# A recurrent cross-attention and maxout kernel on one Trainium2 core: batch 0 loaded uncast on both hardware queues, and every order, bank and queue laid out anew

## The chip, the cores and the metric

The kernel runs on one core of one Trainium2 chip. The metric is the device time of one launch in microseconds (us), the median of several runs. A profiled execution of the same program gives a trace with the busy time of each engine: PE is TensorE (matmuls), PEld its weight loads, DVE is VectorE, ACT is ScalarE, POOL is GpSimd, SP is SyncE (which here only issues DMAs). An engine runs its instructions in the order of the program and waits on semaphores for the others.

## The reference

`x` is 8 x 8 x 512 x 64 (batch, head, position, depth), `state` is 8 x 8 x 32 x 64, both float32. Per batch and head the positions read the states and the states read the positions; then a maxout layer with three weight matrices and an output matrix runs over all 4352 rows.

```python
scores = scale * x @ state.T          # softmax over the 32 states
xread  = softmax(scores) @ state
scores2 = scale * state @ x.T         # softmax over the 512 positions
sread  = softmax(scores2) @ x
rows = concat([xread, sread], axis=2) -> (4352, 512)
h    = maximum(maximum(rows @ w1, rows @ w2), rows @ w3)   # 512 -> 768
out  = h @ w_out                                           # 768 -> 512
```

## The kernel before, in words

Compute is in bfloat16, sums in PSUM are float32. For each batch b the x tile (128 partitions x 2048) is turned so that depth lies on partitions (`xT`), scores of all heads come from matmuls against block diagonals of the states (`bd`), ScalarE takes the exponentials (`e`), VectorE sums and inverts them, and a product gives the weights `a`, which are turned (`aT`). Instead of computing xread and multiplying it with W, the kernel multiplies the states of the batch with W first (`G`, in slices of columns), so that a layer1 product is `aT` times `G`, with 2 contracted blocks. sread is a matmul of `e` with x, is scaled, turned and gathered in `atp`; its rows run through layer 1 at the end for all batches at once ("s").

The whole program is written out by hand as strings of short steps, and each step issues its instructions on a fixed engine in the order of the string. Nothing is rescheduled. FIRST covers batches 0 and 1 and the head of batch 2; EACH is performed for b = 2 to 6, with batch numbers counted from b (`gr 1` is batch b+1, `l2 -1` is batch b-1); LAST ends batches 6, 7 and the states. The letter at the end of a step names the engine that does it or the queue that a DMA goes to (D VectorE, A ScalarE, P GpSimd, S SyncE; two letters: one half each). The steps that matter here:

- loads: `lst k` two batches of states; `lxu b g` one half of the heads of x as float32, uncast, which `cxu` casts afterwards; `lxg b g` the same half cast to bfloat16 by a GpSimd DMA; `lx b` all of x; `lw m0 m1 i` columns 128*m0 to 128*m1 of W number i, cast, GpSimd; `lwo` the output matrix
- `busy n`: n matmuls on zeros; `stc`, `stt`, `stp`: states cast, turned, placed in `bd`, which `clr` clears; `xt`, `xtc`: x turned on TensorE and copied out; `xtd`, `atd`, `srt`: turned by a DMA on SP
- `sc`, `ex`, `sum`, `wt`: scores, exponentials, sums with reciprocal, weights; `at`, `atc`: weights turned and copied; `sr`, `srs`: sread and its scaling (line 323; lines 333 and 339); `pad` a copy of x that sread uses (lines 304 and 307); `ap` places the turned sread in `atp` (`sread_place`, line 347)
- `g`, `gr` with `gc`, `grc`: a slice or run of G columns (line 359) and its copy out (lines 377, 399, 402)
- `l1`: three products of one slice of 128 columns (line 412), into three PSUM banks; `m0` copies the first out on ScalarE (427), `ma` and `mb` take the maxima with the second and third on VectorE (432, 436)
- `l2` with `l2c`: an output block (443, 450); `l2p`, `l2pc`: parts of one (458, 462); `so`, `sop`, `sos`: stores (473, 468 and 466, 481); `look`, `flag`: one flag that says whether all sums lie in a safe range

PSUM has eight banks. Four are handed out singly by the digits of BANKS, in the order of the program, the other four as two pairs by PAIRS; a step that gets a bank waits until the one before it in that bank has been read. At the end the flag is read into a register of every engine, and only if it says that a sum was out of range a second, slower form of the whole computation runs; with these inputs it is skipped.

Of the kernel before, what the change touches and what calls it, by code (L numbers as in the profile page):

```python
# [15 lines left out]


FIRST = """
    zero; busy 10; clr 3; lxu 0 0 S; lxg 1 0; lst 0 A; lxg 0 1; clr 1; busy 1; stc 0 D; clr 0; ident;
    lxg 1 1; busy 2; lw 0 2 1; stt 0; lst 1 S; cxu 0 0 D; xones 0; xt 0 0; stp 0 A; busy 2; xt 1 0;  # L20
    xtc 0 0 D; sc 0 0; busy 4; warm; xtc 1 0 D; lw 0 1 2; xt 0 1; sc 1 0; lw 0 4 0; xt 1 1; ex 0 0;
    xtc 0 1 A; sc 0 1; xones 1; sum 0 0; stc 1 P; ex 1 0; lw 1 3 2; xtc 1 1 D; lw 3 5 2; ex 0 1; lw 2 3 1;
    sum 1 0; sc 1 1; stt 1; busy 6; lw 3 6 1; lxg 2 1; wt 0 0 P; ex 1 1; at 0 0; sum 0 1; sr 0; atc 0 0 A;
    clr 2; busy 1; wt 1 0 P; stp 1 A; wt 0 1 P; at 1 0; sum 1 1; at 0 1; wt 1 1 D; g 0 0; lxg 2 0; sr 1;
    atc 0 1 A; srs 1; at 1 1; g 1 0; g 1 1; gc 0 0 A; atc 1 0 D; l1 0 0; atc 1 1 A; ones; g 0 1; gc 1 0 A;
    gc 1 1 D; m0 0 0; gc 0 1 A; xtd 2; l1 1 0; g 0 2; srs 0; m0 1 0; lw 5 6 0; g 1 2; l1 1 1; ma 0 0;
    lw 5 6 2; lw 4 5 0; l1 0 1; pad 2; mb 0 0; g 1 3; gc 0 2 A; m0 1 1; gc 1 2 A; ma 1 0; lxg 3 1; g 0 3;
    l1 0 2; m0 0 1; gc 0 3 A; m0 0 2; l1 1 2; g 0 4; mb 1 0; g 0 5; ma 1 1; l1 0 3; gc 1 3 A; lst 2 A; lwo;
    mb 1 1; l1 1 3; m0 1 2; ma 0 1; g 1 4; gc 0 4 A; g 1 5; m0 0 3; gc 0 5 A; l1 0 5; mb 0 1; ma 0 2;
    m0 1 3; mb 0 2; gc 1 4 A; m0 0 5; l1 1 4; ma 1 2; mb 1 2; ma 0 3; ma 1 3; l1 0 4; mb 0 3; mb 1 3;  # L30
    ma 0 5; mb 0 5; m0 1 4; m0 0 4; gc 1 5 A; sc 2 -; lxg 3 0; ma 1 4; mb 1 4; gr 2 1024 1280; lst 3 S;
    gr 2 0 512; ex 2 -; xtd 3; l1 1 5; ma 0 4; gr 2 512 1024; grc 2 1024 1280 D; lx 4; gr 2 1792 2304;
    mb 0 4; stc 3 P; sum 2 -; grc 2 0 512 A; grc 2 1792 2304 D; stc 2 P; l2 0 2; m0 1 5; l2 0 3;
    gr 2 1280 1792; l2c 0 2 D; wt 2 - P; stt 2; grc 2 1280 1792 A; l2 0 1; grc 2 512 1024 A; ma 1 5; mb 1 5;
    l2 0 0; stp 2 D; stt 3; sr 2; stp 3 A; l2c 0 3 D; so 0 2 4 A; l2c 0 1 D; l2c 0 0 A; srs 2; so 0 0 2 P;
    atd 2;
"""
EACH = """
    gr 1 1792 2304; lx 3; gr 1 0 512; l2 -1 3; sc 1 -; grc 1 0 512 A; pad 1; l2 -1 0; ex 1 -; l1 0 0;
    l2 -1 1; grc 1 1792 2304 D; gr 1 1280 1792; gr 1 1024 1280; srt -2; xtd 2; sum 1 -; l2c -1 3 A;  # L40
    gr 1 512 1024; sr 1; l2c -1 0 A; m0 0 0; l1 0 1; ma 0 0; l1 0 2; l2c -1 1 A; so -1 0 2 A; mb 0 0;
    grc 1 1024 1280 DA; l1 0 3; srs 1; m0 0 1; m0 0 2; ma 0 1; m0 0 3; mb 0 1; wt 1 - P; l1 0 5; m0 0 5;
    l2 -1 2; grc 1 1280 1792 A; grc 1 512 1024 A; ma 0 2; l1 0 4; mb 0 2; ma 0 3; mb 0 3; ma 0 5; m0 0 4;
    mb 0 5; ma 0 4; mb 0 4; l2c -1 2 A; atd 1; ap -2 D; so -1 2 4 P;
"""
LAST = """
    srt 7; srt 5; l1 7 0; l2 6 3; l1 7 2; ap 5 A; l2 6 1; srt 6; l1 7 3; m0 7 0; ma 7 0; mb 7 0; ap 6 A;
    ap 7 D; m0 7 2; l2c 6 3 D; l2c 6 1 A; l1 7 4; m0 7 3; l1s 0; m0 7 4; ma 7 2; mb 7 2; ma 7 3; mb 7 3;
    l1 7 1; l2 6 0; m0 s 0; ma 7 4; m0 7 1; l2c 6 0 A; ma s 0; mb 7 4; ma 7 1; mb s 0; mb 7 1; l1 7 5;
    m0 7 5; l1s 2; ma 7 5; mb 7 5; m0 s 2; l2p 7 1 384 512; l1s 1; ma s 2; l2p 7 0 384 512; l2p 7 3 256 512;  # L50
    l2pc 7 1 384 512 A; l2 6 2; m0 s 1; sop 7 1 384 512 S; l2p 7 3 0 256; ma s 1; l2p 7 2 128 384;
    l2pc 7 0 384 512 D; l1s 5; l2pc 7 3 256 512 A; l2c 6 2 A; l2p 7 0 0 128; mb s 2; l1s 3; l1s 4; mb s 1;
    l2pc 7 2 128 384 D; m0 s 5; l2p 7 2 0 128; l2p 7 2 384 512; l2p 7 0 128 256; l2pc 7 3 0 256 A;
    l2p 7 1 0 128; m0 s 3; look; ma s 5; sop 7 3 256 512 S; l2pc 7 0 0 128 D; sop 7 2 128 384 S; m0 s 4;
    sop 7 0 384 512 S; mb s 5; sop 7 0 0 128 A; ma s 3; so 6 2 3 P; so 6 1 2 S; so 6 3 4 S; so 6 0 1 P;
    l2pc 7 2 0 128 A; ma s 4; mb s 3; l2p 7 0 256 384; mb s 4; l2pc 7 0 128 256 D; flag; l2p s 0 0 256;
    l2pc 7 2 384 512 A; sop 7 0 128 256 S; sop 7 2 384 512 S; l2pc 7 1 0 128 A; l2pc 7 0 256 384 D;
    l2pc s 0 0 256 D; sop 7 2 0 128 S; l2p 7 1 128 384; l2 s 1; sop 7 1 0 128 A; l2c s 1 D;
    l2pc 7 1 128 384 A; sop 7 3 0 256 S; sop 7 0 256 384 S; sop s 0 0 256 S; sop 7 1 128 384 S;
    l2p s 0 256 512; l2pc s 0 256 512 D; sos 1 A; sop s 0 256 512 S;  # L60
"""

BANKS = """
    0123012130 2310231031 3232132013 2013210321 0321302301 3203123013 0212302131 2031203120 3123013203
    1201320132 0132013210 3120132031 2031203120 3123013203 1201320132 0132013210 3120132031 2031203120
    3123013203 1201321032 0132013021 0230213021 0320323102 3021320130 120312013
"""
PAIRS = """
    0101010110 1010100010 1010010100 1010010100 10
"""  # L70


# [1 line left out]
def kernel(  # L74
# [10 lines left out]
    nc = tc.nc  # L85

    B, H, S, D = x.shape
# [35 lines left out]
    zero = const.tile([128, 512], BF16, name="zero")  # L123
    ident = const.tile([128, 128], BF16, name="ident")
    ones = const.tile([128, 128], BF16, name="ones")
    warm = const.tile([128, 1], F32, name="warm")
# [3 lines left out]
    flag = data.tile([128, 1], I32, name="flag")  # L130

    xT, e, a, aT, G, ht, osb, xp = {}, {}, {}, {}, {}, {}, {}, {}
# [176 lines left out]
    srs = {}  # L309
# [188 lines left out]
    def set_flag():  # L498
# [3 lines left out]
        nc.vector.reduce_sum(out=n, in_=p, axis=AX.X)  # L502
        nc.vector.tensor_scalar(out=flag, in0=n, scalar1=255.5, scalar2=None, op0=ALU.is_le)

# [9 lines left out]
        "gr": (g_run, 1), "grc": (g_ran, 1), "l1": (layer1, 1), "l1s": (layer1_states, 0),  # L517
        "m0": (max_first, 1), "ma": (max_second, 1), "mb": (max_third, 1), "l2": (layer2, 1), "l2c": (layer2_out, 1),
        "l2p": (layer2_part, 1), "l2pc": (layer2_part_out, 1), "sop": (store_part, 1), "so": (store, 1), "sos": (store_states, 0), "look": (look_at_sums, 0), "flag": (set_flag, 0),
    }  # L520

    def value(t):
# [38 lines left out]
    def sread_below_max(b):  # L561
# [18 lines left out]
        for g in range(2):  # L580
            p = bank([128, 2, 2, 128], BF16, "pat")
            for c in range(2):
                for i in range(2):
# [2 lines left out]
                           in_=p.rearrange("p i c k -> p (i c) k"))  # L586
        sread(b)

    bad = nc.values_load(flag[0:1, 0:1], min_val=0, max_val=1,
                         skip_runtime_bounds_check_because="flag is the result of a comparison")  # L590
    homes["b"], homes["w"] = cycle("0123"), cycle("01")
    with tc.If(bad != 0, label="again"):
        for b in range(B):
# [68 lines left out]
```

## Time and profile before

| what | us |
|---|---|
| median of 3 runs (157.18 to 157.36) | 157.34 |
| span of the profiled execution | 155.3 |
| median less span (what lies around it) | 2.04 |
| PE busy / PEld / DVE / ACT / POOL | 147.1 / 73.6 / 113.6 / 87.1 / 52.1 |
| first layer1 matmul, start | 17.02 |
| last matmul, end | about 150.1 |
| landing of the last store | about 154.4 |

The span runs from the first instruction to the last. [...] A window row gives start and end, its length, then busy time and number of instructions of PE, PEld, DVE, ACT and POOL, the granted TensorE clock, the DMA share and the rate in GB/s. A chain row gives the start, the length and what it was. A timeline row gives start, length, engine, line, operation and operands. For a casting load the trace counts the bytes written.

### The profile page before, as it was taken

To read this page: it belongs to the slowest core of one execution; us is meant where nothing else is said; L and a number is where in the kernel's file an instruction comes from. 1 tells how busy PE (TensorE), PEld (TensorE's weight loads), DVE (VectorE), ACT (ScalarE), POOL (GpSimd) and SP (SyncE) were. 2 spreads that over 40 slices of the span, in tenths; PEclk is the share of its full clock that TensorE was granted. 3 is DMA by queue.
4 is the path that set the end of the run, shared out by engine and by line. 5 is a ranking of instruction groups with operands and counts; after the bars stand their busy time and mean duration, and the time that the engine had idled before them with its cause. 6 is when DMAs were issued, how large, how long until landed. Compare 5 with 4: busy or idle time off the path is not lost.

```text
span 155.3 us, 3610 instructions
## 1 busy us (share of the span) xinstructions
PE 147.1 (95%) x1429; PEld 73.6 (47%) x1429; DVE 113.6 (73%) x196; ACT 87.1 (56%) x143; POOL 52.1 (34%) x69
## 2 busy tenths in 40 slices
PE   6989899999999999999999999999999999999960
PEld 2565333354453444444444443444344445679930
DVE  3577788799957788877687799688978767636530
ACT  0677787865486476557655865466637543333300
POOL 6999509502239007700770073106220100002000
PEclk9999999999999999999999999999999999999995
DMA  4999999999979996998499930923060300015444
GB/s 123 231 196 201 196 189 171 159 189 196 194 194 224 268 151 200 130 178 163 153 128 179 177 135 0 174 44 135 4 211 17 135 2 4 0 37 202 167 145 142
DMA packets 39477, 22.30 MB, mean 144 GB/s; under 512 B 23584, under 2 KB 37408, under 8 KB 39456
## 3 DMA queue, kind: packets, MB, share of 16 engines
q0 software_dynamic: 14944, 10.75, 40.5%
q1 hardware_dynamic: 22928, 7.47, 28.2%
q10 hardware_dynamic: 1584, 3.80, 6.8%
q8 instruction: 12, 0.20, 0.5%
q14 instruction: 9, 0.07, 0.2%
HBM read 15.20 MB, written 8.91 MB: 155 GB/s over the span
## 4 chain that ended last, share of the span: by engine, by line
PE 77%; DVE 9%; DMA 6%; POOL 4%; issue 1%; DVEq 0%; POOLq 0%
PE pw L412 45%; PE po L443 19%; DMA w<-in_moe_w_dram 6%; PE pg L359 5%; PE po L458 4%; DVE atp L347 3%; DVE ht L436 2%; PE psr L323 2%; DVE seen L272 1%; DVE G L399 1%; POOL x L166 1%; PE ps L258 1%; POOL w L177 1%; DVE t L432 1%; POOL x L194 1%
## 5 line engine op out<-in xcount | busy, mean ns | idle before, releaser
L412 PE MATMUL pw<-aT,G 128*128 128x512 bf16 x288 | 67.1, 379 | 0.0
L432 DVE TENSOR_TENSOR t<-t,pw 128x512 bf16<-128x512 bf16 (+1 forms) x54 | 35.0, 649 | 14.4 <-ACT t L427 11.8
L427 ACT CAST t<-pw 128x512 bf16<-128x512 f32 (+1 forms) x54 | 30.6, 567 | 23.8 <-PE pw L412 19.9
L412 PEld LDWEIGHTS <-G 128*128 128x128 bf16 x288 | 27.2, 98 | 33.6 <-issue 2.7
L443 PE MATMUL po<-wout,ht 128*128 128x512 bf16 x168 | 40.6, 379 | 0.0
L436 DVE TENSOR_TENSOR ht<-t,pw 128x512 bf16<-128x512 bf16 x48 | 32.9, 686 | 4.8 <-PE pw L412 0.5
L473 POOL DMA_DIRECT2D out_dram<-osb x8 | 4.8, 601 | 66.1 <-ACT osb L450 43.4
L443 PEld LDWEIGHTS <-ht 128*128 128x128 bf16 x168 | 15.3, 98 | 19.3 <-issue 2.3
L399 ACT CAST G<-pg 128x1024 bf16<-128x1024 f32 x18 | 17.7, 1019 | 4.6 <-PE pg L359 4.6
L450 ACT COPY osb<-po 128x512 f32<-128x512 f32 x24 | 13.6, 589 | 10.9 <-PE po L443 10.9
L280 POOL TENSOR_TENSOR a<-e,rden 128x1024 bf16<-128x1024 bf16 (+1 forms) x9 | 14.6, 1636 | 14.4 <-DVE rden L274 6.5
L307 POOL COPY xp<-x 128x1024 bf16<-128x1024 bf16 x12 | 12.4, 1071 | 5.3 <-DMA x<-in_x_dram 5.3
L359 PE MATMUL pg<-w,bd 64*32 64x512 bf16 (+1 forms) x288 | 12.2, 364 | 0.6 <-DMA w<-in_moe_w_dram 0.6
L272 DVE TENSOR_REDUCE seen<-e 128x32 f32<-128x1024 bf16 (+1 forms) x10 | 9.9, 990 | 3.5 <-ACT e L265 3.5
L265 ACT ACTIVATE e<-ps 128x1024 bf16<-128x1024 f32 (+1 forms) x10 | 8.4, 853 | 4.0 <-PE ps L258 2.9
L377 ACT CAST G<-pg 128x768 bf16<-128x768 f32 x11 | 8.9, 808 | 2.9 <-PE pg L359 2.9
L207 PE MATMUL idle<-zero 128*128 128x512 bf16 x26 | 8.5, 472 | 1.3 <-DVE zero L185 1.3
L412 PE MATMUL pw<-atp,w 128*128 128x256 bf16 x72 | 8.7, 273 | 0.0
L359 PEld LDWEIGHTS <-bd 64*32 64x32 bf16 x336 | 3.5, 89 | 9.0 <-issue 7.6
L177 POOL DMA_DIRECT2D w<-in_moe_w_dram x10 | 7.6, 773 | 0.4 <-DMA w<-in_moe_w_dram 0.4
L412 PEld LDWEIGHTS <-w 128*128 128x128 bf16 x72 | 7.0, 98 | 1.2
L347 DVE COPY atp<-ats 128x128 bf16<-128x128 bf16 x6 | 7.5, 1254 | 0.0
(66 smaller groups left out, 111.2 us busy)
## 6 DMA issues: line engine op xcount, KB each, us to landing
out_dram<-osb ACTq DMA_DIRECT2D x6, 512.0 KB, 5.0
out_dram<-osb POOLq DMA_DIRECT2D x6, 512.0 KB, 3.0
x<-in_x_dram POOLq DMA_DIRECT2D x4, 512.0 KB, 8.1
x<-in_x_dram POOLq DMA_DIRECT2D x7, 256.0 KB, 5.9
w<-in_moe_w_dram POOLq DMA_DIRECT2D x3, 256.0 KB, 9.2
wout<-in_moe_w_out_dram POOLq DMA_DIRECT2D x1, 768.0 KB, 9.4
out_dram<-osb SPq DMA_DIRECT2D x6, 128.0 KB, 3.0
w<-in_moe_w_dram POOLq DMA_DIRECT2D x5, 128.0 KB, 8.4
```

The lines of the kernel that those rows point to most:

```text
L272: nc.vector.reduce_sum(out=den, in_=parity(e[b], g), axis=AX.X)
L280: times[c](out=parity(a[b], g).rearrange("p j g s n -> p j (g s) n"), in0=parity(e[b], g).rearrange("p j g s n -> p j (g s) n"), in1=rdens ...
L307: nc.gpsimd.tensor_copy(out=xp[b][:, :, :, g * (D + 1):g * (D + 1) + D], in_=v[:, g])
L347: copier[c](out=atp[:, :, b // 4, :, b % 4], in_=ats[:, b])
L359: nc.tensor.matmul(p(s, g), bd(b, 2 * s + g)[64 * g:64 * g + 64, g, :], f(w_sb[64 * g:64 * g + 64, s]), start=True, stop=True, tile_positi ...
L399: copier[c[g]](out=v[:, g:h], in_=p[:, g:h, 0:c1 - c0])
L412: nc.tensor.matmul(pw[i][:, 0:n], lhs(i, k), rhs(k), start=(k == 0), stop=(k == nk - 1))
L427: nc.scalar.copy(out=t0s[b, m][:, 0:n], in_=open_ps["l", b, m][0][:, 0:n])
L432: nc.vector.tensor_max(t1s[b, m][:, 0:n], t0s.pop((b, m))[:, 0:n], open_ps["l", b, m][1][:, 0:n])
L436: nc.vector.tensor_max(ht[b][:, m, :], t1s.pop((b, m))[:, 0:n], open_ps.pop(("l", b, m))[2][:, 0:n])
L443: nc.tensor.matmul(p, ht[b][:, m, j * 128:(j + 1) * 128], wout_sb[:, m, :], start=(m == 0), stop=(m == NM - 1))
L450: copier[c[i]](out=o[:, j, i * w:i * w + w], in_=p[:, i * w:i * w + w])
```

## The change

Batch 0's x is no longer loaded half uncast by SP and half cast by GpSimd: both halves come uncast, one on SP's queue and one on ACT's, and GpSimd casts the second. W is loaded in column slices 0 and 1 of all three matrices, then 2 and 3, then 4 and 5, and the first loads of it lie between the two halves of batch 1's x. `ident` comes first on GpSimd. All orders of FIRST, EACH and LAST, the engine of many copies, the queues of stores, and the lists of banks and pairs are new. In EACH, `ap` goes from VectorE to ScalarE, `so -1 0 2` from ACT's queue to POOL's, and layer1's slices 1, 2, 3, 5 and 4 follow each other without a layer2 step between them. `l1 0 0 1` and `l1 1 3 1` run the three products of a layer1 slice interleaved instead of one after another. The reading of the flag becomes a step of its own (`vl`), ahead of SP's last two stores.

The diff, cut: the head of FIRST, the whole of EACH, the end of LAST, and the new step.

```diff
 FIRST = """
-    zero; busy 10; clr 3; lxu 0 0 S; lxg 1 0; lst 0 A; lxg 0 1; clr 1; busy 1; stc 0 D; clr 0; ident;
-    lxg 1 1; busy 2; lw 0 2 1; stt 0; lst 1 S; cxu 0 0 D; xones 0; xt 0 0; stp 0 A; busy 2; xt 1 0;
-    xtc 0 0 D; sc 0 0; busy 4; warm; xtc 1 0 D; lw 0 1 2; xt 0 1; sc 1 0; lw 0 4 0; xt 1 1; ex 0 0;
-    xtc 0 1 A; sc 0 1; xones 1; sum 0 0; stc 1 P; ex 1 0; lw 1 3 2; xtc 1 1 D; lw 3 5 2; ex 0 1; lw 2 3 1;
-    sum 1 0; sc 1 1; stt 1; busy 6; lw 3 6 1; lxg 2 1; wt 0 0 P; ex 1 1; at 0 0; sum 0 1; sr 0; atc 0 0 A;
-    clr 2; busy 1; wt 1 0 P; stp 1 A; wt 0 1 P; at 1 0; sum 1 1; at 0 1; wt 1 1 D; g 0 0; lxg 2 0; sr 1;
-    atc 0 1 A; srs 1; at 1 1; g 1 0; g 1 1; gc 0 0 A; atc 1 0 D; l1 0 0; atc 1 1 A; ones; g 0 1; gc 1 0 A;
-    gc 1 1 D; m0 0 0; gc 0 1 A; xtd 2; l1 1 0; g 0 2; srs 0; m0 1 0; lw 5 6 0; g 1 2; l1 1 1; ma 0 0;
...
+    ident; zero; busy 1; lxg 1 0; lw 0 2 2; lst 0 A; busy 1; lxu 0 1 A; clr 0; busy 1; lxg 1 1;
+    lxu 0 0 S; cxu 0 0 D; busy 2; lw 0 2 1; clr 2; clr 1; busy 1; stc 0 A; busy 1; lst 1 S; busy 1;
+    cxu 0 1 P; busy 1; xones 1; busy 1; stt 0; busy 1; xt 0 0; busy 1; stp 0 A; lw 0 2 0; lw 2 4 2;
+    busy 1; busy 1; xtc 0 0 DA; xt 0 1; xt 1 0; xtc 0 1 D; xones 0; sc 0 0; busy 1; stc 1 A; sc 0 1;
+    ex 0 0; lw 2 4 1; busy 2; busy 1; xtc 1 0 D; stt 1; ex 0 1; sum 0 0; sum 0 1; lw 2 4 0; wt 0 0 P;
+    busy 1; sc 1 0; wt 0 1 P; busy 1; stp 1 A; xt 1 1; ex 1 0; sr 0; xtc 1 1 DA; busy 1; warm; at 0 0;
+    sum 1 0; busy 1; busy 1; srs 0; wt 1 0 D; lxg 2 0; at 0 1; sc 1 1; busy 1; g 0 0; busy 1; g 0 1;
+    atc 0 0 A; atc 0 1 A; ex 1 1; gc 0 0 DA; gc 0 1 D; sum 1 1; at 1 0; wt 1 1 P; l1 0 0 1; atc 1 0 D;
+    g 1 0; g 1 1; m0 0 0; ma 0 0; l1 0 1; at 1 1; mb 0 0; gc 1 0 A; sr 1; m0 0 1; ma 0 1; g 1 2;
+    atc 1 1 D; gc 1 1 A; gc 1 2 A; g 0 2; lw 4 6 0; l1 1 0; m0 1 0; lxg 2 1; mb 0 1; l1 1 1; g 0 3;
+    gc 0 2 DA; m0 1 1; g 1 3; gc 0 3 A; l1 0 2; lw 4 6 2; srs 1; ma 1 0; l1 1 2; l1 0 3; m0 0 2; ma 1 1;
+    lw 4 6 1; mb 1 1; mb 1 0; g 0 4; ma 0 2; lst 2 A; g 0 5; m0 1 2; pad 2; ones; mb 0 2; gc 1 3 A;
+    ma 1 2; lst 3 A; m0 0 3; l1 1 3 1; gc 0 4 A; xtd 2; lwo; mb 1 2; g 1 5; ma 0 3; gc 0 5 DA; mb 0 3;
...
 EACH = """
-    gr 1 1792 2304; lx 3; gr 1 0 512; l2 -1 3; sc 1 -; grc 1 0 512 A; pad 1; l2 -1 0; ex 1 -; l1 0 0;
-    l2 -1 1; grc 1 1792 2304 D; gr 1 1280 1792; gr 1 1024 1280; srt -2; xtd 2; sum 1 -; l2c -1 3 A;
-    gr 1 512 1024; sr 1; l2c -1 0 A; m0 0 0; l1 0 1; ma 0 0; l1 0 2; l2c -1 1 A; so -1 0 2 A; mb 0 0;
-    grc 1 1024 1280 DA; l1 0 3; srs 1; m0 0 1; m0 0 2; ma 0 1; m0 0 3; mb 0 1; wt 1 - P; l1 0 5; m0 0 5;
-    l2 -1 2; grc 1 1280 1792 A; grc 1 512 1024 A; ma 0 2; l1 0 4; mb 0 2; ma 0 3; mb 0 3; ma 0 5; m0 0 4;
-    mb 0 5; ma 0 4; mb 0 4; l2c -1 2 A; atd 1; ap -2 D; so -1 2 4 P;
+    l2 -1 1; l2 -1 0; l2c -1 0 A; lx 3; gr 1 0 512; gr 1 1792 2304; l1 0 0; pad 1; grc 1 0 512 D;
+    sc 1 -; l2 -1 3; grc 1 1792 2304 A; gr 1 1280 1792; m0 0 0; gr 1 1024 1280; gr 1 512 1024; srt -2;
+    ex 1 -; sr 1; ma 0 0; l2c -1 1 A; mb 0 0; l2c -1 3 A; sum 1 -; so -1 0 2 P; srs 1;
+    grc 1 1024 1280 A; l1 0 1; l1 0 2; m0 0 1; l1 0 3; wt 1 - P; grc 1 512 1024 DA; l1 0 5; m0 0 2;
+    ma 0 1; mb 0 1; xtd 2; ma 0 2; m0 0 3; mb 0 2; m0 0 5; ma 0 3; l1 0 4; mb 0 3; ma 0 5; m0 0 4;
+    ap -2 A; ma 0 4; l2 -1 2; mb 0 5; atd 1; mb 0 4; l2c -1 2 A; so -1 2 4 P; grc 1 1280 1792 AD;
 """
 LAST = """
...
-    l2pc 7 2 384 512 A; sop 7 0 128 256 S; sop 7 2 384 512 S; l2pc 7 1 0 128 A; l2pc 7 0 256 384 D;
-    l2pc s 0 0 256 D; sop 7 2 0 128 S; l2p 7 1 128 384; l2 s 1; sop 7 1 0 128 A; l2c s 1 D;
-    l2pc 7 1 128 384 A; sop 7 3 0 256 S; sop 7 0 256 384 S; sop s 0 0 256 S; sop 7 1 128 384 S;
-    l2p s 0 256 512; l2pc s 0 256 512 D; sos 1 A; sop s 0 256 512 S;
+    l2c 6 0 D; mb s 4; l2 s 1; look; l2p 7 2 384 512; l2pc 7 3 256 512 D; flag; l2c s 1 A;
+    l2p s 0 256 512; sop 7 0 128 256 P; l2p s 0 0 256; l2p 7 1 128 384; l2p 7 2 0 128;
+    l2pc 7 2 384 512 D; sop 7 3 0 256 S; l2pc s 0 256 512 D; l2p 7 0 384 512; l2p 7 2 128 384;
+    sop 7 3 256 512 A; l2pc s 0 0 256 A; l2pc 7 1 128 384 D; sop 7 2 384 512 A; sop s 0 256 512 A;
+    l2pc 7 2 0 128 D; l2p 7 1 384 512; l2pc 7 0 384 512 D; sop 7 2 0 128 A; l2pc 7 1 384 512 D;
+    so 6 0 1 S; sop 7 0 384 512 A; l2pc 7 2 128 384 A; sop 7 2 128 384 A; sop 7 1 384 512 A; so 6 3 4 P;
+    sos 1 S; vl; sop s 0 0 256 S; sop 7 1 128 384 S;
 """
...
+    bads = []
+
+    def read_flag():
+        bads.append(nc.values_load(flag[0:1, 0:1], min_val=0, max_val=1,
+                                   skip_runtime_bounds_check_because="flag is the result of a comparison"))
...
+        "vl": (read_flag, 0),
...
-    bad = nc.values_load(flag[0:1, 0:1], min_val=0, max_val=1,
-                         skip_runtime_bounds_check_because="flag is the result of a comparison")
+    bad = bads[0]
```

The singles that EACH takes in the new list, for b = 4: layer2 3 1 and 3 0 [2] [0]; layer1 4 0 [1, 3, 0]; layer2 3 3 [1]; run 1024 [3, 0]; sread [2]; layer1 slices 1, 2, 3, 5, 4 [1, 3, 0] [2, 1, 3] [2, 0, 1] [2, 3, 0] [2, 1, 3]; layer2 3 2 [2]. Pairs: runs 0, 1792, scores, runs 1280, 512 take 0, 1, 0, 1, 0.

## The prediction, made before the changed kernel had run

> **What bounds the kernel now.** I read the page first, then the chain in order of time, the stage windows, and timelines of the start, one steady batch and the end.
>
> The page:
>
> ```profile
> span 155.3 us, 3610 instructions
> PE 147.1 (95%) x1429; PEld 73.6 (47%) x1429; DVE 113.6 (73%) x196; ACT 87.1 (56%) x143; POOL 52.1 (34%) x69
> PEclk9999999999999999999999999999999999999995
> PE 77%; DVE 9%; DMA 6%; POOL 4%; issue 1%; DVEq 0%; POOLq 0%
> ```
>
> TensorE (PE) is busy 95% of the span at full granted clock; only its gaps can be won. The chain, in order of time, shows where they are:
>
> ```profile
> 7.43 9.26 DMA w<-in_moe_w_dram
> ...
> 16.73 0.36 PE pg L359 x8
> 17.09 1.40 PE pw L412 x6
> ...
> 90.62 2.16 DVE atp L347
> ...
> 149.48 0.69 DVE osb L450
> 150.17 0.39 DVE osb L462
> ```
>
> Until 16.7 the kernel waits for loads, W last. From then to about 150.1 the chain is almost all PE, but for two VectorE (DVE) detours. The windows, one for each of the five EACH batches (start and length in the first columns), size them:
>
> ```profile
> 43.54:58.78 15.24, 15.24 (x156) 6.88 (x149) 10.65 (x19) 10.75 (x18) 5.48 (x6) 1.00 1.21 215
> 58.78:74.03 15.25, 15.25 (x149) 6.83 (x148) 12.36 (x20) 9.70 (x16) 5.61 (x6) 1.00 0.95 171
> 74.03:89.28 15.25, 15.25 (x150) 6.84 (x149) 11.56 (x20) 9.70 (x16) 5.51 (x6) 1.00 0.88 159
> 89.28:105.44 16.16, 15.88 (x149) 6.80 (x148) 13.32 (x20) 9.70 (x16) 4.63 (x5) 1.00 0.39 85
> 105.44:121.20 15.76, 15.48 (x150) 6.99 (x150) 13.29 (x20) 9.68 (x16) 4.62 (x5) 1.00 0.27 90
> ```
>
> Three batches take 15.25; the last two lose 0.91 and 0.51. The timeline says to what: the sread_place copy (`ap`) beside POOL's `pad` copies.
>
> ```profile
> 75.29 0.30 DVE L347 COPY atp<-ats 128x128 bf16<-128x128 bf16 x1
> ...
> 90.54 2.24 DVE L347 COPY atp<-ats 128x128 bf16<-128x128 bf16 x1
> 90.56 2.05 POOL L307 COPY xp<-x 128x1024 bf16<-128x1024 bf16 x2
> ```
>
> So the end is: start (17.0) + PE work with few gaps (133.1) + tail (155.3 - 150.1 = 5.2). The median of 157.34 is 2.04 above the span; I leave that part as it is. The plan's PE work is the same before and after except for idle fillers: the same layer1, layer2, g and l2p pieces stand in both. I therefore sum four terms.
>
> **Start.** How fast loads go, in 40 slices of the first 20 us:
>
> ```profile
> GB/s 0 0 0 23 164 129 344 391 379 265 194 195 176 193 194 195 201 192 196 195 181 196 210 205 207 211 192 198 196 215 186 193 179 192 202 205 199 199 195 196
> ```
>
> The float32 loads of SP and ACT write 344 to 391 GB/s; casting loads then write 195, which is 390 read. So read bytes are the limit, about 0.385 MB/us from 2.0 on. Test: `lw 0 4 0`, with 4.19 MB read up to and including it, comes to 12.9 and landed at 13.9; `lw 1 3 2`, with 4.72 MB, comes to 14.3 and landed at 16.7. A landing is thus 1.0 to 2.4 behind the sum. The new plan has 3.93 MB up to the last of W's slices 0 and 1 (`lw 0 2 0`): 12.2, landing between 13.2 and 14.6. W comes 2 to 3 us earlier.
>
> But it is no longer what ends last. Two uncast halves (0.5 MB each) and the states come first on both hardware queues, so x0's first half lands near 5.9 instead of 4.9 and its second near 6.8. POOL casts that one: 1.2 (twice the 0.62 of its 128x512 casts), to 8.0. Queued behind it on POOL stand `xones`, four W loads at 0.75 each and `xones` (to 11.45), then `wt 0 0` and `wt 0 1` at 1.08 (3.1 for three now), to 13.55. PE needs both: at 0 1, sc 1 1, g 0 0 at 14.5, g 0 1, half a gc each on two engines (0.5), layer1 0 0 at about 15.7 instead of 17.02. That is 1.3 earlier, but at 1 1 (0.23), sr 1 (0.5) and one g (0.3) are still to do, which is 1.0. **Term: -0.3**; bounds -1.3 (POOL's wait short) to +0.9 (x0 or W one more microsecond late).
>
> The rows show the hardware loads going ahead of POOL's: POOL's first x load, issued at 1.37, landed at 6.6. [...] The 344 to 391 GB/s slices do not look interleaved.
>
> One more price: the L194 memset on POOL took 0.64 beside the DVE cast at 4.93 and 0.18 alone later. The new POOL cast may meet DVE's x cast and two clears (0.69, 0.5, 0.5), so it may be up to 0.8 late; I count none, since the clear at 4.09 ran beside POOL's load issue at 3.57 and lengthened neither.
>
> **Rest of FIRST.** `lw 4 6` now stands behind `wt 1 1` on POOL (18.45, after sum 1 1), so the queue runs dry from about 17.7 to 20; its last part lands near 26.6 (four 0.52 MB reads at 1.36, plus 1.2). g 0 4 comes at about 27.3: 0.7 spare. DVE now takes half of gc 0 2 and gc 0 5 (0.5 each) between max pairs. **Term: +0.2**; bounds 0 to +1.2.
>
> **The five batches.** I lay the new EACH order out with today's pitches, from l2 -1 1 at 0: l2 and l1 1.29, two gr 0.56, l1 after gr 1.31, sc 0.46, three gr 0.67, sr 0.38, 0.10 issue before each g stage. Then l1 0 is at 3.24, sc 4.55, l2 -1 3 5.01, sr 7.07, l1 1 7.45, then 2, 3, 5, 4 at 8.74, 10.04, 11.33, 12.63, l2 -1 2 13.92, end 15.21 if nothing waits (15.25 now).
>
> ScalarE: grc 1792 A 3.37 to 4.39, m0 0 to 4.88, ex 5.27 to 6.29. DVE: ma 0 4.91, mb 0 5.69, sum at 6.33 (after ex), reciprocal 7.59 (+1.26), srs 7.85 (+0.26) and 8.05 (+0.20), half of grc 512 8.25, ma 1 8.86 (+0.61), done 9.55. By the bank list layer1 2's third product (7.45 + 2.16 = 9.60) needs that bank: on time by 0.05. Today ma 1 begins 1.26 after layer1 1 (66.14 to 67.40); here 1.41. A max pair takes DVE 1.39 (67.40 to 68.80) and a layer1 PE 1.29, and five now follow each other without a layer2 between: 0.09, 0.19, 0.28 are lost by the last. So 15.49 a batch, 77.45 for five against 77.66 now.
>
> In this the `ap` copy moves from DVE to ScalarE, where it took 0.49; the two losses (1.42) go, and the creep (1.4) takes their place. ScalarE then waits for products in l1's run anyway (idle 0.7 at each m0 now), which covers the 0.49. `so -1 0 2` moves to POOL ahead of `wt`; its data is out at 6.8 and wt's reciprocal at 7.9, so wt is not late; without that cover wt would wait and with it `atd` (5.4 to landing, 3 us spare). l2 -1 1 needs max 4 done at 16.05, and reaches that operand at 16.35. **Term: -0.2**; bounds -1.6 (no creep) to +1.5 (ma 1 0.3 later each time).
>
> **LAST and the tail.** Six layer1 and six layer1_states with maxes laid out the same way give waits of 0.1 at most: 0. Now the last store starts 0.96 after PE's end, behind another on SP, lands 3.3 later and the span ends 0.94 after that:
>
> ```profile
> 151.06 0.56 SPq L466 DMA_DIRECT2D out_dram<-osb  x1
> ...
> out_dram<-osb SPq DMA_DIRECT2D x1, 128.0 KB, 3.3
> ```
>
> In the new order the last pieces are small and go out by ACT: sop 7 2 128 384 at about +0.2 (copy 0.37 after a product that ends 0.33 before PE's end) and sop 7 1 384 512 at +0.6. With 3.1 to 3.9 to land, as SP's 128 KB late stores, the tail is 4.2 to 5.0. The read of the flag moves ahead of SP's last two stores; no row prices it. Today it fits between the last issue (151.62) and the landing (154.36), so it is below 2.7 and hidden; moved, it stands where SP waits for data. **Term: -0.7**; bounds -0.95 to +0.3.
>
> Sum: -0.3 + 0.2 - 0.2 - 0.7 = -1.0, so **156.3**.
>
> **Rivals.**
>
> Slower, VectorE becomes the bound of the batches (0.22): if ma 1 starts over 1.46 after layer1 1, every batch loses the difference on top of the creep. For: five layer1 in a row, sum and srs and a cast directly ahead of ma 1. Against: DVE is busy only 10.7 to 12.4 of 15.25 in clean batches. With 0.35 late, 15.84 a batch, 79.2, +1.5 in place of -0.2: 158.0.
>
> Late third W slices (0.15): the transposing load of x 2 runs beside `lw 4 6`, as between 22 and 26 now, where the rate fell to 151 GB/s. Then g 0 4 waits 1.0 to 1.5: +0.9 beyond the forecast, and more if layer1 follows: 157.4.
>
> The start works as its order intends (0.15): POOL's wt is early and W's 13.2 decides: layer1 0 0 at 14.7, term -1.3, total -2.0: 155.3. The 0.64 memset and POOL's row of issues speak against it.
>
> The forecast has 0.48; alone it spans 155.7 to 156.9. A measurement of this kernel can tell about 0.2% (0.3 us) from no change. Faster: 0.42 of the forecast plus 0.15, 0.57. Same: 0.04, 0.07 of the late slices, 0.02 of the first rival: 0.13. Slower: 0.02, 0.08 and 0.20: 0.30. The range over these cases is 155.0 to 158.2.
>
> **What would show it.** Layer1 0 0 at 15 to 16.5 with POOL's wt 0 1 or ACT's aT copy ahead of it, not W; batches of 15.3 to 15.7, all five alike, with PE's short waits on DVE's maxes inside the layer1 run; L347 on ScalarE at 0.5; last landing 3.2 to 4.1 after PE's end. Wrong: a DMA wait before layer1 0 0 or at g 0 4 over 0.5, batches over 15.7 or at 15.25, or a tail as long as 5.2.

## The result, and the profile after

The changed kernel takes **163.06 us** (median of 4 runs, 162.09 to 165.01), the kernel before 157.26 beside it (156.79 to 157.36): a ratio of **1.0361 [1.0305, 1.0417]**. The forecast was 156.3, range 155.0 to 158.2: wrong, in sign too. Ratios leave out slow executions, those over 1.5% above the fastest of their kernel, and the profiled execution of the changed kernel, at 165.01, is one of these. So the trace below shows a loss of 7.8 us of span where the medians show 5.8; the kinds of loss are read from it, and its sizes are held against other kernels' traces further down.

The page: span, busy times, granted clock in 40 slices, and the chain by engine.

```profile
span 163.1 us, 3632 instructions
...
PE 150.3 (92%) x1428; PEld 74.6 (46%) x1428; DVE 113.9 (70%) x203; ACT 86.1 (53%) x155; POOL 52.9 (32%) x71
...
PEclk9999999786999999999999999999999999999996
...
PE 76%; DMA 17%; POOL 2%; DVE 1%; issue 0%; ACTq 0%; ACT 0%; SPq 0%; POOLq 0%
```

Two things are new. The clock row dips in slices 8 to 10 (about 28 to 41 us), where it was even; and DMA holds 17% of the chain, where it was 6%. The chain in order of time (start, length, what) says which transfers:

```profile
18.57 0.76 POOL w L179
19.33 5.49 DMA x<-in_x_dram
24.89 13.37 DMA xT<-x
38.31 1.04 PE ps L260 x16
39.34 3.45 PE pw L414 x12
...
155.46 2.29 DMA out_dram<-osb
```

From 19.3 to 38.3 the end hangs on batch 2's x: its second half is loaded (5.5 us) and then turned by the transposing load `xtd 2` (13.4 us, where the same load took 5.0 before). The view of the DMA issues has both, before first (the last number is us from issue to landing):

```profile
xT<-x SPq DMA_TRANSPOSE x1, 5.0
...
xT<-x SPq DMA_TRANSPOSE x1, 13.4
```

TensorE's timeline shows how that looks from its side (start, length, instruction, and in brackets the idle time just before and its releaser):

```profile
15.63 1.46 PE L414 MATMUL pw<-aT,G 128*128 128x512 bf16 x6
...
29.40 0.52 PE L361 MATMUL pg<-w,bd 64*32 64x384 bf16 x16 [1.96 <-DMA w<-in_moe_w_dram]
...
38.31 1.04 PE L260 MATMUL ps<-bd,xT 128*128 128x64 bf16 x16 [3.56 <-DMA xT<-x]
39.16 3.64 PE L414 MATMUL pw<-aT,G 128*128 128x512 bf16 x12
```

The first layer1 starts at 15.63, 1.4 earlier than before. Then `g 0 4` waits 1.96 for W's last slices (`lw 4 6`), `sc 2` waits 3.56 for `xtd 2`, and the twelve matmuls behind it take 3.64 where twelve take 2.77 at full clock. The windows hold the same by stage (start and end, length, busy time of PE, PEld, DVE, ACT, POOL, granted clock, DMA share, GB/s); the last two are steady batches:

```profile
15.63:29.40 13.77, 11.81 (x129) 4.96 (x127) 11.43 (x21) 8.38 (x14) 9.48 (x13) 1.00 1.17 136
29.40:38.30 8.90, 5.35 (x44) 1.53 (x44) 4.24 (x7) 3.87 (x6) 0.61 (x1) 0.77 1.38 118
38.30:53.50 15.20, 15.19 (x148) 7.22 (x149) 10.18 (x17) 7.99 (x13) 4.34 (x5) 0.91 1.08 207
68.97:84.40 15.43, 15.43 (x150) 6.88 (x149) 12.05 (x19) 9.53 (x17) 5.78 (x8) 1.00 0.73 157
84.40:99.83 15.43, 15.43 (x150) 6.87 (x149) 12.05 (x19) 9.53 (x17) 6.33 (x9) 1.00 0.71 156
```

The loss lies in the first three rows: the first holds the wait of 1.96, in the second TensorE is busy for 5.35 of 8.90 us at a mean clock of 0.77, and in the third the mean clock is 0.91. The clock's records show two stretches of 3.413 us at half rate, from 30.7 and from 37.5. What stood on POOL, whose queue issues these loads, was this:

```profile
17.53 1.04 POOL L282 TENSOR_TENSOR a<-e,rden 128x512 bf16<-128x512 bf16 x1 [3.14 <-DVE rden L276]
18.53 0.81 POOL L179 DMA_DIRECT2D w<-in_moe_w_dram  x1
19.33 0.75 POOL L168 DMA_DIRECT2D x<-in_x_dram  x1
20.06 1.50 POOL L179 DMA_DIRECT2D w<-in_moe_w_dram  x2
```

POOL waits 3.14 us for `wt 1 1`'s reciprocal; only behind that come W's last slices and the second half of x 2. All of them land late and together: the two last W loads 7.8 and 8.5 us after issue, and `xtd 2` runs beside them, beside the states' loads of ScalarE's queue, and then beside wout (26.0), x 3 and x 4 (26.8 to 29.2).

Part of this belongs to the one execution. The rate of all queues together, in 40 slices from 20 to 45 us:

```profile
GB/s 47 75 219 180 195 184 150 166 180 198 256 169 77 13 19 162 194 181 157 64 50 52 71 55 43 61 115 206 207 209 214 193 196 194 190 194 180 183 186 187
```

It fell to 13 and 19 GB/s from 28.1 to 29.4 and to 43 to 71 from 31.9 to 36.3, with issued loads still to land. The kernel with fillers (below) issues the same loads in the same order, 0.3 to 0.4 earlier; its queues moved 201 and 196 GB/s in those two stretches, W's last slice landed 7.0 us after its issue instead of 8.5, and `xtd 2` 7.9 after instead of 13.4. Why the rate fell here stays open.

### The profile page after: what moved, and what is told of

Same layout as the page of the kernel before. It is cut to its first block, busy times and chain, and to the rows that moved or that the text cites. A ratio compares the mean times of both kernels' runs of the same rounds, so it can differ in the third digit from the quotient of the medians.

```text
span 163.1 us, 3632 instructions
## 1 busy us (share of the span) xinstructions
PE 150.3 (92%) x1428; PEld 74.6 (46%) x1428; DVE 113.9 (70%) x203; ACT 86.1 (53%) x155; POOL 52.9 (32%) x71
## 4 chain that ended last, share of the span: by engine, by line
PE 76%; DMA 17%; POOL 2%; DVE 1%; issue 0%; ACTq 0%; ACT 0%; SPq 0%; POOLq 0%
PE pw L414 38%; PE po L445 23%; DMA xT<-x 8%; PE pg L361 4%; DMA osb<-in_x_dram 4%; DMA x<-in_x_dram 3%; PE ps L260 3%; PE po L460 3%; PE psr L325 2%; PE idle L209 2%; DMA out_dram<-osb 1%; PE pxt L235 1%; POOL x L176 1%; POOL a L282 1%; DVE G L379 1%; PE pgh L361 0%
## 5 line engine op out<-in xcount | busy, mean ns | idle before, releaser
L414 PE MATMUL pw<-aT,G 128*128 128x512 bf16 x288 | 69.4, 388 | 0.0
L414 PEld LDWEIGHTS <-G 128*128 128x128 bf16 x288 | 27.1, 99 | 37.0 <-issue 9.4
L445 PE MATMUL po<-wout,ht 128*128 128x512 bf16 x168 | 38.7, 379 | 0.0
L445 PEld LDWEIGHTS <-ht 128*128 128x128 bf16 x168 | 16.0, 98 | 18.3 <-DVE ht L438 0.2
L475 POOL DMA_DIRECT2D out_dram<-osb x12 | 6.9, 574 | 51.6 <-ACT osb L452 47.4
L401 DVE CAST G<-pg 128x512 bf16<-128x512 f32 (+1 forms) x17 | 14.3, 845 | 9.3 <-PE pg L361 5.0
L401 ACT CAST G<-pg 128x512 bf16<-128x512 f32 (+1 forms) x19 | 14.1, 745 | 3.0 <-DVE G L401 2.9
L209 PE MATMUL idle<-zero 128*128 128x512 bf16 x25 | 9.6, 491 | 1.3 <-DVE zero L187 1.3
L379 ACT CAST G<-pg 128x768 bf16<-128x768 f32 (+1 forms) x11 | 7.8, 716 | 5.3 <-PE pg L361 5.0
L260 PE MATMUL ps<-bd,xT 128*128 128x64 bf16 x128 | 5.8, 199 | 3.6 <-DMA xT<-x 3.6
L260 PEld LDWEIGHTS <-xT 128*128 128x128 bf16 x128 | 5.2, 102 | 5.5 <-DMA xT<-x 4.1
```

Of the source, the lines that this page charges most:

```text
L209: nc.tensor.matmul(p, zero[:, 0:128], zero, start=True, stop=True)
L260: nc.tensor.matmul(p[:, 2 * jj:2 * jj + 2, k - gs[0], s, :], xT[b][:, 2 * s + k, jj, :], bd(b, 2 * s + k).rearrange("p c n -> p (c n)"), s ...
L401: copier[c[g]](out=v[:, g:h], in_=p[:, g:h, 0:c1 - c0])
L414: nc.tensor.matmul(pw[i][:, 0:n], lhs(i, k), rhs(k), start=(k == 0), stop=(k == nk - 1))
L445: nc.tensor.matmul(p, ht[b][:, m, j * 128:(j + 1) * 128], wout_sb[:, m, :], start=(m == 0), stop=(m == NM - 1))
```

## The experiments

Every kernel is the changed kernel ("after") with the edit shown; times stand against the kernel before, on the same chip. In what was expected, "theory" is: the loads that stand late on POOL's queue and the transposing load on SP's hold each other up, and the waits then cost clock too. Where an edit adds steps that take a PSUM bank, or puts in another list, the list of banks follows.

**W's last slices early.**

```
-    ... g 0 2; lw 4 6 0; ...   l1 0 2; lw 4 6 2; ...   lw 4 6 1; mb 1 1; ...
+    ... wt 1 0 D; lxg 2 0; lw 4 6 0; lw 4 6 2; lw 4 6 1; at 0 1; ...
```

> The changed kernel with one move: the three loads of W's slices 4 and 5 stand on POOL directly behind lxg 2 0, ahead of wt 1 1 and lxg 2 1, instead of behind them. Theory (the transposing load of x 2 collides with W's last loads, because those were issued only after wt 1 1 and a dry queue): W's slices 4 and 5 land near 23, no wait at g 0 4 (2.0 before), x 2's second half lands near 24.5 and the transposing load after it runs with little beside it, 5 to 6 us to landing instead of 13.4; no half clock; about 157. Rival 1 (the states' loads on ACT's queue slow the transposing load) and rival 2 (the output matrix and x 3, x 4, issued right behind, slow it): the 2.0 at g 0 4 go, the transposing load still takes 11 to 14 and the scores of batch 2 wait 3 to 5; 160 to 161.

Measured: 160.17 (158.74 to 160.88), ratio 1.0175 [1.011, 1.0239]. The wait for W is gone; the one for the transposing load is not:

```profile
32.86 0.83 PE L261 MATMUL ps<-bd,xT 128*128 128x64 bf16 x16 [2.14 <-DMA xT<-x]
33.50 4.26 PE L415 MATMUL pw<-aT,G 128*128 128x512 bf16 x12
```

This is TensorE's timeline again: 2.14 of waiting, then twelve matmuls at 4.26, inside a half-clock stretch that begins at 33.1. So moving W gives back about half of the loss (1.9 of 3.6% by the ratios), and the wait for the transposing load remains.

**The states' loads early** (they ran beside both).

```
-    ... ma 0 2; lst 2 A; g 0 5; ...   ma 1 2; lst 3 A; m0 0 3; ...
+    ... m0 0 1; lst 2 A; lst 3 A; ma 0 1; ...
```

> The changed kernel with lst 2 and lst 3 issued on ACT's queue at about 18 (behind m0 0 1), while POOL's queue is dry, instead of 24.0 and 25.3. Rival 1 (the states' loads slow the transposing load): transposing load 5 to 7 us to landing, W's last part no later than 28, 157 to 159. Theory and rival 2: nothing changes but a few tenths, 162 to 164, transposing load 11 to 14 us.

Measured: 161.79 (161.19 to 162.32), ratio 1.0295 [1.0259, 1.0331]. `g 0 4` waits 0.80 and `sc 2` 2.55, and the clock is halved once (from 34.4). Moving the states' loads gives back 0.7% by the ratios, so they are not the cause by themselves.

**wout, x 3 and x 4 held back until the transposing load has landed**, by a copy of one column on POOL that reads its result.

```
-    ... xtd 2; lwo; mb 1 2; ...
+    ... xtd 2; hold 2; lwo; mb 1 2; ...
+    def hold(b):
+        nc.gpsimd.tensor_copy(out=held, in_=xT[b][:, 0, 0, 0:1])
```

> The changed kernel with one small POOL copy out of xT of batch 2 ahead of lwo, so that the loads of the output matrix, x 3 and x 4 are issued only when the transposing load of x 2 has landed. Rival 2 (those later loads slow it): the transposing load lands 6 to 8 us after issue, at about 31 to 33, the wait of the scores goes; the output matrix lands near 40 and layer2 may wait for it; 158 to 161. Theory: the collision with W's last loads is there as before, W late as before (2.0 at g 0 4), the transposing load at most 2 us faster, and what is behind it later: 162 to 165.

Measured: 161.36 (160.53 to 163.35), ratio 1.0304 [1.0237, 1.037]. `xtd 2` lands after 5.8 us, `sc 2` does not wait, and the clock stays full. The expected 2.0 at `g 0 4` did not come, though the loads ahead of `xtd 2` are the same; and wout, now issued at 31, is what comes late:

```profile
27.80 0.52 PE L368 MATMUL pg<-w,bd 64*32 64x384 bf16 x16 [0.26 <-DMA w<-in_moe_w_dram]
...
39.39 5.35 PE L452 MATMUL po<-wout,ht 128*128 128x512 bf16 x24 [2.55 <-DMA wout<-in_moe_w_out_dram]
```

`g 0 4` waits 0.26: W's lateness of 1.96 is not in every execution of these loads. Layer2 waits 2.55 for wout: the wait moved one load down the queue.

**Both: W early and the loads behind held back.** The two edits above together.

> The kernel w_early with the POOL copy of hold ahead of lwo: W early, and nothing issued behind the transposing load until it has landed. If the loads behind it hold up its landing (7.7 us in w_early, of which the data took 3), it lands 5 to 5.8 us after its issue, near 30.5, and the scores of batch 2 wait 0.3 at most instead of 2.1; the output matrix is then issued at 30.5 and layer2 waits 0 to 2 for it; 157.3 to 158.8 against 160.2. If they do not, landing stays at 7 to 8 and the time at 160 or above.

Measured: 160.21 (160.15 to 160.28), ratio 1.0193 [1.0162, 1.0224]. The transposing load is at its quickest (issued at 25.19, landed 4.4 later) and neither W nor it makes TensorE wait; POOL's and then TensorE's timeline show the price:

```profile
29.69 0.19 POOL L191 COPY held<-xT 128x1 bf16<-128x1 bf16 x1 [3.32 <-DMA xT<-x]
...
37.97 5.35 PE L452 MATMUL po<-wout,ht 128*128 128x512 bf16 x23 [1.76 <-DMA wout<-in_moe_w_out_dram]
```

wout is late by 1.76, and the transposing load behind layer1's weights (`aT`) by 1.84 later. Against W early alone it gains nothing. In each of these kernels x 2's second half is loaded from 18 or 19 to 25, and in each one of the loads that follow is late.

**Fillers for the clock** (idle matmuls where TensorE waits).

```
-    ... g 0 4; ...            sc 2 -; ...
+    ... busy 5; g 0 4; ...    busy 16; sc 2 -; ...
```

> The changed kernel with matmuls on zeros where PE waits: 5 ahead of g 0 4 and 16 ahead of the scores of batch 2. It measures the half clock alone: if the two stretches of half clock (30.7 to 34.1 and 37.5 to 41.0) come from PE's idle time, they vanish and 2 to 2.5 us with them, about 160.7, with both DMA waits as they were. If the half clock costs nothing (its matmuls would have waited for the loads anyway), 163 or more, by the fillers' own time.

Measured: 161.48 (160.96 to 161.93), ratio 1.0275 [1.0243, 1.0308]: 1.6 below the changed kernel's median (1.4 by the two ratios), with no half-clock stretch left. That does not price the clock. W's last slice had landed at 27.35 and `xtd 2` at 32.44 (7.9 after issue), while the fillers kept TensorE until 28.41 and 35.59: some 4 us of this execution are the fillers' own.

**x 2 turned by TensorE**, without the transposing load.

```
-    ... xtd 2; lwo; ...   g 1 4; gc 1 4 A; l1 0 5; m0 0 5; sc 2 -; ... l1 1 4; ...
+    ... lwo; ...          g 1 4; xt 2 0; xtc 2 0 A; ... xt 2 1; xtc 2 1 A; ... l1 1 4; sc 2 -; ...
```

> The changed kernel with x 2 turned by 16 matmuls on PE and two copies on ScalarE instead of the transposing load (scores of batch 2 one layer1 later). It takes the transposing load out of the collision. Theory: W's slices 4 and 5, still issued late, land near 26.5 to 27.5, a wait of 0 to 0.5 at g 0 4, no wait for xT, no half clock; PE has 1.2 more to do; 157.5 to 158.5. If W is late by its own issue alone, g 0 4 still waits 1 to 2 and the half clock stays: 159.5 to 161.

Measured: 161.43 (161.15 to 161.72), ratio 1.0274 [1.0247, 1.0301]. The total decides nothing, since my edit brought waits of its own (1.36 for a bank, 1.47 and 0.35 for ScalarE's copies) and 1.2 of matmuls. Nor does the row that was to decide: `g 0 4` waits 0.39 for W, as forecast, and W's last slice lands 6.9 after its issue; but with the transposing load beside it that slice landed 6.8 (held back) and 7.0 (fillers) after. That the transposing load holds W up is not shown.

**All of x 2 and of W early.**

```
-    ... g 0 2; lw 4 6 0; ...  lxg 2 1; ...  lw 4 6 2; ...  lw 4 6 1; ...
+    ... wt 1 0 D; lxg 2 0; lxg 2 1; lw 4 6 0; lw 4 6 2; lw 4 6 1; at 0 1; ...
```

> The changed kernel with both halves of x 2 and then W's slices 4 and 5 on POOL directly behind wt 0 1, so that x 2 lands near 20 and its transposing load is issued then, beside W's last loads but long before the output matrix's. Theory as it stands after the first four runs (W late because issued late; the transposing load's landing held up by the loads issued behind it, the output matrix first): W lands near 25 to 27 and x 2 is turned near 27, both before they are needed (27.4 and 31), no half clock, FIRST ends near 43.5, about 157.0 (156.6 to 157.6). Rival (any load beside a transposing one slows both): W at 28 or later, waits of 1 to 3 in FIRST, 158 to 160.

Measured: 156.48 (156.05 to 157.95, 10 runs), ratio 0.9974 [0.9944, 1.0003]. Only four loads changed place, and by the two ratios some 6 us are back. The chain of this run, for the stretch that held the DMA lines above:

```profile
27.25 0.45 PE pg L362 x16
27.70 1.40 PE pw L415 x6
29.10 0.45 PE pg L362 x16
29.55 1.40 PE pw L415 x6
30.95 0.47 PE ps L261 x16
31.42 2.62 PE pw L415 x12
```

PE from end to end, at full clock. The transposing load is not quick here either (issued at 20.79, landed 8.6 later, at 29.3); it is early, 1.4 before `sc 2` starts. So it is the order of these four loads that turned the forecast over; the rest of the plan stayed as it was.

**x 2 early alone**, W left where it was.

```
-    ... lxg 2 0; at 0 1; ...           m0 1 0; lxg 2 1; mb 0 1; ...
+    ... lxg 2 0; lxg 2 1; at 0 1; ...  m0 1 0; mb 0 1; ...
```

> Batch 2's second half is loaded right behind its first; the three loads of W's last slices keep their places behind the last weights on POOL's queue. That fills in the fourth corner of a square: neither load early (after, 163.06), W early (160.17), both early (156.48). Theory (the transposing load and the loads around it hold each other up, and the transposing load comes first on that chain): issued near 20.8, the transposing load is through before the scores of batch 2 at about 30.8, which do not wait; W is late by its own late issue only, so that g 0 4 waits 0.3 to 1.0 and the granted clock stays full; the span is 155.0 to 156.0 and the time 156.8 to 157.8. Rival (W late at g 0 4 is what starts the loss, whatever the transposing load does): g 0 4 waits 1.5 to 2.5 as in after, half clock follows, and the time is 159 or more.

Measured: 158.95 (156.73 to 160.79), ratio 1.0077 [0.9999, 1.0154]. The execution that was profiled took 156.73 and has no wait for W or for x 2 at all (theory had 0.3 to 1.0 for W); its margin is thin: `xtd 2` lands at 30.8 (9.9 after issue) and `sc 2` starts at 31.16. The other runs of it took 158.84 and more. That they are those in which one of the two loads misses its turn fits the margin, but there is no trace of them: this corner of the square stays open. Moving W as well widens the margin to 1.4 and narrows the spread, from 4.1 us over four runs to 1.9 over ten.

**Which of the three lists is worth what.** First, x 2 and W early, with LAST as before:

> The same with LAST of the kernel before (the flag read at the end). If the new LAST cost 0.25 in its tail, as the two traces say, 0.2 to 0.3 below the kernel without this; if the new tail gives the 0.7 that the prediction counted whenever the run is undisturbed, 0.5 to 0.9 above it.

Measured: 157.44 (156.12 to 158.17), ratio 1.0016 [0.9992, 1.0041]. From batch 7's scores to TensorE's end it needs 40.88 in place of 40.01, with tails alike (5.51 and 5.58). So behind the new EACH the new LAST is worth 0.9 by this stretch (0.7 by the two ratios), where I had it the other way about: none in LAST itself, all in the tail. Second, FIRST as before, with the new EACH and LAST:

> FIRST of the kernel before with EACH and LAST of the changed one: the two terms of the prediction behind the start, by themselves. By the traces the five batches give 0.3 and the tail takes 0.25: 157.0 to 157.4, no difference that can be told. By the prediction's terms (0.2 and 0.7): 156.3. If EACH needs FIRST's new end (which bank and which pair stand last), 158 or more.

Measured: 157.74 (157.38 to 158.27), ratio 1.0039 [1.0022, 1.0056]. From the end of the first `sr 2` to batch 3's scores it takes 5.17, 0.68 more than with the new FIRST (4.49), and 0.61 of that is layer2's wait for VectorE: the old list ends in another state than the new EACH begins with. EACH and LAST alone therefore bring nothing.

**One cast of a steady batch from VectorE to ScalarE**, on top of x 2 and W early.

```
-    ... wt 1 - P; grc 1 512 1024 DA; l1 0 5; ...
+    ... wt 1 - P; grc 1 512 1024 A; l1 0 5; ...
```

> The kernel x2_first with one letter less in EACH: grc 1 512 1024 all on ScalarE instead of half on VectorE. It tests how the prediction explained the batches (VectorE's chain reaches the first maximum of layer1 1 just too late, and five layer1 in a row lose up to 0.1 each). If so, that maximum comes 0.3 earlier, the creep nearly goes, batches take 15.22 to 15.32 instead of 15.43, and the time falls by 0.5 to 1.0 against x2_first (156.5): 155.5 to 156.0. Rival (the 0.2 over 15.21 is a fixed cost, such as PE's issue between steps): batches stay at 15.43, or grow if ScalarE becomes late for m0.

Measured: 156.17 (155.5 to 157.65, 12 runs), ratio 0.9935 [0.991, 0.996]. The windows of two steady batches:

```profile
62.30:77.66 15.36, 15.26 (x148) 6.88 (x148) 11.56 (x18) 9.83 (x18) 6.07 (x8) 1.00 0.73 156
77.66:93.02 15.36, 15.26 (x148) 6.89 (x149) 11.57 (x18) 9.83 (x18) 5.26 (x7) 1.00 0.70 155
```

A batch takes 15.36 instead of 15.43, less than was expected: this cast on VectorE is a third of the 0.22 over 15.21, and what holds the rest is not shown. The intervals of the two kernels overlap, so the gain in time is not shown by itself.

**The last stores in another order**, on top of that: two 64 KB stores from ScalarE's queue to the end of SP's.

```
-    ... sop 7 2 0 128 A; ... sop 7 0 384 512 A; ... sop 7 1 128 384 S;
+    ... sop 7 1 128 384 S; sop 7 2 0 128 S; sop 7 0 384 512 S;
```

> The same, and two late stores (sop 7 2 0 128 and sop 7 0 384 512) taken from ACT's queue to the end of SP's, because in the changed kernel ACT stood at their issue, waiting for VectorE's copies, while its own last copy could have begun (157.35 possible, 157.74 done). If ACT's row of issues made the tail long, the span's end comes 0.2 to 0.5 nearer to PE's end (5.4 to 5.6 now); if the landing of whatever is last decides, nothing changes, or SP's own issues (0.35 to 0.67 each) make it longer.

Measured: **155.86** (155.7 to 156.16), ratio **0.9919 [0.9894, 0.9943]**, the best of all, below both kernels; the interval overlaps that of the kernel it builds on, so the stores' own share is not shown. The tail of the profiled execution did not get shorter (5.60, 5.35 before the edit): ScalarE issues its last store 0.35 earlier against TensorE's end, and the late 64 KB stores land 3.8 after issue instead of 3.2.

## Why the prediction was wrong, step by step

**Start, -0.3: right, as far as it was measured.** The first layer1 was forecast for 15.7 and came at 15.63, with POOL's and the casts' chain ahead of it and not W: POOL's two weights were done at 13.63, 13.55 in the sum. The x halves landed at 5.3 and 7.3, 5.9 and 6.8 in the sum, and W's slices 0 and 1 at 13.8, 13.2 to 14.6 in the sum (whose lower bound rests on `lw 0 4 0` landing at 13.9; it was 14.1). The 1.0 of work that was left over behind this point was not measured by itself, and the start varies by more than the term (below), so its size may be luck.

**Rest of FIRST, +0.2 (bounds 0 to +1.2): the step that failed.** The sum put no price on the transposing load `xtd 2`, whose landing behind x 2's late half then held `sc 2`. With the start at -0.3, the batches at -0.3, LAST at 0 and the tail at +0.2, the span's 7.8 leave about +8.2 for it. Against the kernel with x 2 and W early, which does the same work, the trace splits the loss: 1.96 at `g 0 4`, 3.56 at `sc 2`, 1.7 for the first half-clock stretch (half of 3.413, through which TensorE was mostly busy) and 1.0 from the scores of batch 2 to those of batch 3 (17.59 against 16.55), where the second stretch lies; together 8.2, and the spans differ by 8.4. These sizes are of the one execution; by the times, moving W gives back about half of the loss, and moving W and x 2 all of it. The term priced `lw 4 6` alone: four reads one after another, landing at 26.6. They landed at 29.3 here, and at 27.1 to 28.0 in the five other kernels that leave W where it was. It saw that the queue runs dry behind `wt 1 1`, but not that what then stands in it is issued into the same few us as ScalarE's and SP's loads. And it had three gaps:

- `xtd 2` was never costed. Its issue moved from 23.24 to 24.89, and the sum has no price for its landing beside what would now run with it. That landing took 13.4 here, and 7.7 (W early), 7.9 (fillers) and 9.0 (states early) in the others that issue it near 25 with loads close behind, where it took 5.0 before. In the runs with W and with the states early `sc 2` waits 2.14 and 2.55 for it.
- The rival of the late slices had the right pair (the transposing load of x 2 beside `lw 4 6`), and its wait at `g 0 4` was too short for this execution (1.0 to 1.5 forecast, 1.96 measured) and too long for others (0.26 held back, 0.80 states early). It counted the delay of W's side only, which is not shown to come from the transposing load; the longer wait was on the other side, at `sc 2`.
- Nothing in the sum priced a wait beyond its own length. Here two waits brought 2.7 us more in lost clock, by my estimate (the 1.7 and 1.0 above).

**The five batches, -0.2: right.** 15.43, 15.42, 15.43 and 15.49 against 15.49; five take 77.36 against 77.45. `ap` runs on ScalarE at 0.48, the two losses beside `pad` are gone, and every batch has a creep of 0.21 to 0.28 over 15.21 where 0.28 was forecast; the run with one cast moved ties some 0.07 of it to VectorE. The rival that had VectorE as the bound (15.84 a batch) did not come.

**LAST, 0: right in sum** (28.91 after, 28.90 before, from EACH's end to TensorE's). But behind the new EACH the old LAST takes 0.9 more, which I had not foreseen; whether the new one is better or only fits the new EACH is not shown.

**The tail, -0.7 (bounds -0.95 to +0.3): mis-sized,** +0.2. The last stores should have been issued at +0.2 and +0.6 after TensorE's end. ScalarE's queue and ScalarE itself were behind:

```profile
157.74 0.37 ACT L464 COPY osb<-po 128x256 f32<-128x256 f32 x1 [1.96 <-DMA out_dram<-osb]
158.14 0.82 ACTq L470 DMA_DIRECT2D out_dram<-osb  x2
```

TensorE ends at 157.68; the two last issues begin at 158.14 and 158.58. From 156.72 to 157.70 ScalarE stood in two issues, the first of which waited for VectorE's copies, so the stores that were moved to it delayed its own last copy. Then landings of 3.3 and 1.2 to the span's end: 5.42. The bounds of 4.2 to 5.0 were added up wrong: they are those of the store at +0.2, and the last one, at +0.6, would have given 4.6 to 5.4, for a term between -0.6 and +0.2.

## What the runs showed of the hardware

**In these traces `xtd 2` landed 1.6 to 4.9 us after its last packet where packets of large loads behind it had begun before, and 0.5 to 1.0 after it where none had.** From the packet records of the traces, for `xtd 2` (us after its issue):

| kernel | last packet | landing | between | large loads behind it on POOL's queue: first issue, first packet |
|---|---|---|---|---|
| before | 4.0 | 5.0 | 1.0 | x, wout, two x: 2.0, 4.1 |
| after | 11.8 | 13.4 | 1.6 | wout, three x: 1.1, 5.7 |
| W early | 4.3 | 7.7 | 3.4 | wout, three x: 1.1, 4.0 |
| states early | 4.1 | 9.0 | 4.9 | wout, three x: 1.1, 4.0 |
| fillers | 5.4 | 7.9 | 2.4 | wout, three x: 1.1, 5.3 |
| x 2 and W early | 5.5 | 8.6 | 3.1 | wout, three x: 1.1, 5.3 |
| x 2 early | 7.8 | 9.9 | 2.0 | wout, three x: 2.3, 7.0 |
| held back | 5.3 | 5.8 | 0.5 | none |
| W early, held back | 4.0 | 4.4 | 0.5 | none |

In all but two the data is moved within 4 to 5.5 us. With nothing large behind, the landing follows in 0.5; in the kernel before, where the first packet behind moved only when the transposing load's last was through, in 1.0; where packets behind had begun before, in 1.6 to 4.9. The two kernels with W early are the clean pair: the data takes 4.3 and 4.0, and with the loads behind held back the landing comes after 4.4 instead of 7.7. In the changed kernel this tail is the smaller part, since the data itself took 11.8. What holds the landing back is not shown.

**Half clock followed idling of 1.96 to 2.79 us in one window of 3.413.** Both stretches at half clock inside the changed kernel (from 30.71 and from 37.54) are 3.413 us long, and its changes of clock, at 6.82, 30.71, 34.13, 37.54, 40.95 and 160.42, lie 7, 1, 1, 1 and 35 times that apart; those of the kernel before, at 5.39 and 152.16, lie 43 times that apart. I counted the idling in windows of this grid. The stretch followed a window with 1.96 or 2.79 (after), 2.14 (W early) or 2.55 us (states early) of waiting in it; and in the kernel before, whose last matmul ends at 150.09, the half clock that begins at 152.16 follows a window with 2.06. None followed where a wait fell across two windows, as the 2.55 for wout (1.2 and 1.4; held back), nor after the 1.76 for wout in one window (W early, held back). That the place of a wait on the grid counts beside its length fits all of these; what lowers the clock is not shown.

**The start is not the same twice.** The four kernels with x 2 and W early have the same FIRST, and their profiled executions reached the first layer1 at 14.99, 15.05, 15.44 and 15.75. A term of 0.3 in the start is within that.

## What to carry to other kernels

When a load is moved, lay out every load that will be in flight with it, on all queues, and ask of each when it must have landed; a transposing load wants to be issued early enough to take twice its quiet time (4.4 us quiet here, 7.7 to 9.9 with large loads begun behind it, 13.4 once). Where a wait is likely, price it with the clock: waits of 1.96 and 3.56 us each came with 3.413 us at half clock here, which I put at up to 1.7 more. One profiled execution can have a wait that others of the same order lack (for W at `g 0 4`, 1.96 in the changed kernel and 0.26 with the loads behind held back), so a cause read from it is worth a second trace. And an order of work that is right on paper for the engines can lose or win several per cent by the place of four loads in one queue (a ratio of 1.0361 here, 0.9974 with those four moved).
